# A late slot of at most 32 tokens, taken out of the list and computed in plain float32 beside another slot

## The chip, the cores and the metric

The kernel runs on one core of a Trainium2 chip. The metric is the device time of one execution in microseconds. Five engines work beside each other: PE (matrix products, with PEld loading the stationary operands), DVE, ACT and POOL (vector, activation and general work), and SP, whose queue issues most of the DMAs.

## The reference

An attention without a square of scores, whose output feeds a mixture of eight experts with one expert for each token. The batch is 8, with 8 heads, 576 positions and 64 channels a head, so 4,608 tokens of 512 channels.

```python
q_s = softmax(q, axis=-1);  k_s = softmax(k, axis=2)
kv = np.einsum('bhsd,bhse->bhde', k_s, v)
x = np.einsum('bhsd,bhde->bhse', q_s, kv)        # -> (4608, 512)
logits = xn @ en.T / tau                          # x and expert_emb normalized
expert_idx = np.argmax(logits, axis=1)
gate_w = softmax(logits)[arange(N), expert_idx]
for e in range(8):
    mask = expert_idx == e
    h = np.maximum(x[mask] @ w1[e], 0.0)          # w1[e]: 512 x 1024
    out[mask] = gate_w[mask, None] * (h @ w2[e])  # w2[e]: 1024 x 512
```

`softmax` stands for the exponentials less their maximum over their sum plus 1e-9. How many tokens an expert has is known only while the kernel runs.

## The kernel before

**Attention and routing.** Four groups of two batches are worked through in an order of small steps that is written out by hand (`ORDER`); each step is emitted when its name comes up, and every engine runs its own steps in that order. Step names that begin with `lp` are the instructions of the late plan, one DVE instruction each.

**Slots.** The tokens of one expert are computed in slots. Two direct slots and four early ones, 256 tokens each, run while the attention is still going on. What is left then is computed in late slots of up to three tiles of 128 tokens, expert after expert. The late plan (`late_plan`, lines 874 to 966) counts what each expert has left (`rem`), the tiles that make it up (`tiles`), the slots that these need (`ns`, tiles by three, rounded up), and for each slot in the list its expert, its first row and its count (`par`). An expert with a single token left has one tile and so one slot. The number of slots is `total`; the loop (lines 1373 to 1421) skips those behind it.

**One late slot.** Its products are made in split precision: every operand is cast to a rounded high part (ACT, line 1137) and a rest (DVE, line 1139), and three products of these stand for one. The first layer (`ffn1`, lines 1185 to 1187) runs over four quarters of the hidden units with 384 columns, or 256 where the slot has at most two tiles; 24 products a quarter. ACT and DVE (lines 1190 and 1192) make the two parts of the hidden values. The second layer (`ffn2`, lines 1207 to 1209) is 24 products of 512 columns for each tile that the slot has. ACT scales with the gate (line 1219) and POOL scatters the rows to the output (line 1221).

**What a slot prepares.** `fetch(...)[4]` is a row of functions: `[5]` reads the next slot's x rows in pieces (line 1088), `[7]` its first weights in four loads (line 1116), `[3]` its second weights in four (line 1126), `[4]` fills rows behind an expert's last one (line 1076). There is one buffer for raw first weights and one for raw second weights. So the first weights of the next slot are asked for when this slot's have all been split, ahead of its start; the second weights of the next slot go out one by one, as this slot's are split in its first layer. `split1` and `turnx` (block transposes of the x rows on DVE, and their split) are in `prepare` and `hidden`.

**PSUM in the late part.** Two buffers of tag `t`, two of `x` (first layer) and two of `po` (second layer).

Of the kernel before, what the change touches and what calls it, by code (L numbers as in the profile page):

```python
# [9 lines left out]
F32 = mybir.dt.float32  # L10
F32R = mybir.dt.float32r
BF16 = mybir.dt.bfloat16
I32 = mybir.dt.int32
# [10 lines left out]
P = 128  # L24
# [30 lines left out]
NMIN = -(-(N - TOOK_MAX) // T)  # L55
# [68 lines left out]
s4.3 lp6.3 lp7.3 lp9.3 lp8.3 gD.3 lp0.3 lp10.3 lp36.3 gE.3 s5.3 lp12.3 lp13.3 s6.3 lp29.3 pa43.4 lp11.3 lp14.3 lp15.3  # L124
lp16.3 lp17.3 pa42.4 pb42.4 hl41.4 hh42.4 hl42.4 pb43.4 hh43.4 hl43.4 lp18.3 lp19.3 lp20.3 lp21.3 lp22.3 lp23.3 lp27.3
lp37.3 lp25.3 lp26.3 lp28.3 lp30.3 lp35.3 lp24.3 lp33.3 lp31.3 lp34.3 sc6.3 po40.4 x5p1.4 sc3.3 od30.4 ob40.4 sc2.3
sc1.3 od31.4 sc7.3 sc4.3 lp32.3 sc8.3 sc5.3 x5p0.4 sc0.3 po41.4 x5h0.4 x5h1.4 ob41.4 od41.4 od40.4 x5l1.4 x5l0.4
right.4
# [4 lines left out]
def attention_moe(ctx, tc, q, k, v, emb, tau, w1, w2, out):  # L133
# [740 lines left out]
    def late_plan():  # L874
# [21 lines left out]
        st, ct = of_s[:, 2:3], of_s[:, 3:4]  # L896
        total = t([1], "total", I32)
# [7 lines left out]
        def spread():  # L905
# [15 lines left out]
            lambda: DVE.tensor_copy(ns, ni),  # L921
            lambda: DVE.scalar_tensor_tensor(nfull, ns, float(1 - TS), tiles, ALU.mult, ALU.add),
# [8 lines left out]
            lambda: DVE.tensor_tensor(i, slot_f, of_s[:, 0:1], ALU.subtract),  # L931
# [11 lines left out]
            lambda: DVE.tensor_scalar(bad, es, float(E), float(2 * ROWS), ALU.is_ge, ALU.mult),  # L943
            lambda: DVE.tensor_tensor(left, left, bad, ALU.add),
# [97 lines left out]
    def fetch(s, plan, i):  # L1042
# [30 lines left out]
        def pad():  # L1073
# [123 lines left out]
    def ffn2(s, j, got, bank="po", cuts=()):  # L1197

        ix = got[0]
        hh, hl = h_t["e" if s < EARLY - 1 else "l"]  # L1200
        ts_ = slice(j * P, (j + 1) * P)
        po = ps.tile([P, 2 * DM if bank == "x" else DM], F32, tag=bank, name=f"po{s}_{j}")[:, :DM]
        for c in range(NF):
            if c in cuts:
                yield
            for u in range(2):
                PE.matmul(po, hh[c][:, u, ts_], w2h[c][:, u, :], start=c + u == 0, stop=False)  # L1207
                PE.matmul(po, hh[c][:, u, ts_], w2l[c][:, u, :], start=False, stop=False)  # L1208
                PE.matmul(po, hl[c][:, u, ts_], w2h[c][:, u, :], start=False, stop=c + u == NC2 // 2)  # L1209
        yield  # L1210

        tag, bufs = ("et", 3) if s >= EARLY - 1 else (("mt", "kvd")[j], 1)
        ob = wk.tile([P, DM], F32, tag=tag, bufs=bufs, name=f"ob{s}_{j}")
# [17 lines left out]
        yield  # L1231

# [137 lines left out]
    got, total = last_early(), plans[-1][2]  # L1370
    open_banks("late")
    with ExitStack() as ifs:
        for s in range(EARLY, SLOTS):
# [80 lines left out]
```

## Time and profile before

| | |
|---|---|
| median of three runs | 588.98 us (584.9 to 590.15) |
| the profiled execution | 591.84 us |
| its span, first to last instruction | 590.0 us |
| mean granted clock of PE | 0.974 |
| PE busy | 531.2 us, 90% of the span |
| DVE, ACT, POOL busy | 352.2, 281.0, 204.4 us |
| expert weights loaded (`r`) | 96 loads of 512 KB |
| late tiles, of all 38 scattered | 26 |

How to read it. Times in the rows are microseconds from the span's start, if they are not marked ns. `L1185` is line 1185 of the kernel. PE's matmuls are pipelined: the start-to-start distance is the pace, and the duration of one is longer. A row of the timeline gives the start, the duration, the line and engine, the operation, out and in, and in brackets the idle time before it and what ended it. Where equal instructions follow one another, one row merges them (x64).

### The profile page before, as it was taken

To read this page: it belongs to the slowest core of one execution; us is meant where nothing else is said; L and a number is where in the kernel's file an instruction comes from. 1 tells how busy PE (TensorE), PEld (TensorE's weight loads), DVE (VectorE), ACT (ScalarE), POOL (GpSimd) and SP (SyncE) were. 2 spreads that over 40 slices of the span, in tenths; PEclk is the share of its full clock that TensorE was granted. 3 is DMA by queue.
4 is the path that set the end of the run, shared out by engine and by line. 5 is a ranking of instruction groups with operands and counts; after the bars stand their busy time and mean duration, and the time that the engine had idled before them with its cause. 6 is when DMAs were issued, how large, how long until landed. Compare 5 with 4: busy or idle time off the path is not lost. (4 is left out here: it accounts for less than half of the span.)

```text
span 590.0 us, 13113 instructions
## 1 busy us (share of the span) xinstructions
PE 531.2 (90%) x5068; PEld 476.3 (81%) x5068; DVE 352.2 (60%) x612; ACT 281.0 (48%) x423; POOL 204.4 (35%) x205
## 2 busy tenths in 40 slices
PE   1587887977599799999999998999999999999995
PEld 0476876876499687989998887989898989989894
DVE  4989989874465435644474758645547373645560
ACT  3459576724366426414453546344445353444450
POOL 1536428567248382174304133021131303031101
PEclk9989899989889999999999999999999999999998
DMA  9966925567563422059989687985674948485100
GB/s 317 391 222 203 323 86 183 170 214 255 201 189 107 154 91 75 2 209 308 281 261 207 204 197 209 254 187 189 158 218 121 240 127 229 140 198 188 46 19 33
DMA packets 65140, 109.23 MB, mean 185 GB/s; under 512 B 9918, under 2 KB 30942, under 8 KB 65056
## 3 DMA queue, kind: packets, MB, share of 16 engines
q1 hardware_dynamic: 55776, 85.76, 50.2%
q0 software_dynamic: 9200, 22.36, 11.0%
q8 instruction: 50, 0.82, 0.6%
q14 instruction: 34, 0.28, 0.2%
q10 hardware_dynamic: 80, 0.02, 0.0%
HBM read 88.66 MB, written 27.33 MB: 197 GB/s over the span
## 5 line engine op out<-in xcount | busy, mean ns | idle before, releaser
L1139 DVE TENSOR_TENSOR weights<-r,weights 128x1024 fp32r<-128x1024 f32 x92 | 117.3, 1291 | 72.5 <-ACT weights L1137 71.5
L1221 POOL DMA_INDIRECT out_dram<-ob,ix x34 | 37.2, 1095 | 241.8 <-ACT ob L1219 217.7
L1137 ACT CAST weights<-r 128x1024 fp32r<-128x1024 f32 x96 | 98.5, 1043 | 13.8 <-DMA r<-in_moe_w_dram 11.0
L1185 PE MATMUL ph<-x,weights 128*128 128x384 f32 (+1 forms) x320 | 102.3, 320 | 2.3 <-ACTq L1417 1.3
L1187 PE MATMUL ph<-x,weights 128*128 128x384 f32 (+1 forms) x320 | 102.2, 319 | 0.6 <-DVE weights L1139 0.6
L1186 PE MATMUL ph<-x,weights 128*128 128x384 f32 (+1 forms) x320 | 102.1, 319 | 0.1
L1208 PE MATMUL po<-weights,h_l 128*128 128x512 f32 x224 | 87.3, 390 | 0.0
L1209 PE MATMUL po<-weights,h_l 128*128 128x512 f32 x224 | 87.3, 390 | 0.0
L1207 PE MATMUL po<-weights,h_l 128*128 128x512 f32 x224 | 87.3, 390 | 0.0
L1192 DVE SCALAR_TENSOR_TENSOR h_l<-ph,h_l 128x768 fp32r<-128x768 f32 (+1 forms) x44 | 37.8, 860 | 47.7 <-ACT h_l L1190 47.4
L1190 ACT ACTIVATE h_l<-ph 128x768 fp32r<-128x768 f32 (+1 forms) x44 | 32.3, 734 | 66.4 <-PE ph L1187 58.1
L1185 PEld LDWEIGHTS ph<-x,weights 128*128 128x128 f32 x320 | 60.5, 189 | 3.6 <-ACTq L1417 1.7
L1185 PE MATMUL ph<-weights 128*128 128x256 f32 x192 | 58.1, 302 | 3.6 <-DVE h_most L1192 3.3
L1187 PEld LDWEIGHTS ph<-x,weights 128*128 128x128 f32 x320 | 60.5, 189 | 1.0 <-DVE weights L1139 1.0
L1186 PEld LDWEIGHTS ph<-x,weights 128*128 128x128 f32 x320 | 60.5, 189 | 0.5 <-issue 0.3
L1186 PE MATMUL ph<-weights 128*128 128x256 f32 x192 | 56.8, 296 | 1.7 <-issue 1.7
L1219 ACT ACTIVATE ob<-po,ix 128x512 f32<-128x512 f32 x34 | 23.3, 685 | 66.9 <-PE po L1209 53.3
L1209 PEld LDWEIGHTS po<-weights,h_l 128*128 128x128 f32 x224 | 42.0, 188 | 8.7
L1207 PEld LDWEIGHTS po<-weights,h_l 128*128 128x128 f32 x224 | 42.1, 188 | 8.5
L1208 PEld LDWEIGHTS po<-weights,h_l 128*128 128x128 f32 x224 | 42.1, 188 | 8.5
L819 POOL DMA_INDIRECT x_by_e<-x,posu x36 | 37.1, 1030 | 30.5 <-issue 8.1
L1187 PE MATMUL ph<-weights 128*128 128x256 f32 x144 | 42.7, 297 | 0.9 <-DVE weights L1139 0.9
(318 smaller groups left out, 957.0 us busy)
## 6 DMA issues: line engine op xcount, KB each, us to landing
r<-in_moe_w_dram SPq DMA_DIRECT2D x96, 512.0 KB, 6.8
k<-in_k_dram SPq DMA_DIRECT2D x6, 1152.0 KB, 7.9
q<-in_q_dram SPq DMA_DIRECT2D x6, 1152.0 KB, 5.3
v<-in_v_dram SPq DMA_DIRECT2D x6, 1152.0 KB, 13.3
xq<-x_by_e SPq DMA_DIRECT2D x36, 192.0 KB, 3.6
left<-in_v_dram SPq DMA_DIRECT2D x2, 1152.0 KB
left<-in_q_dram SPq DMA_DIRECT2D x2, 1152.0 KB, 10.9
left<-in_k_dram SPq DMA_DIRECT2D x1, 1152.0 KB, 7.8
```

The costliest lines, as they stand in the source:

```text
L819: ins = POOL.indirect_dma_start(x_by_e, bass.IndirectOffsetOnAxis(ap=posu[:, c : c + 1], axis=0), buf["x", g][:, j].bitcast(I32), None, bo ...
L1137: ACT.copy(hi, src)
L1139: eng.tensor_tensor(lo, src, hi.bitcast(F32), ALU.subtract)
L1185: PE.matmul(o, w1h[c][:, d, fs], xh[:, d, :n], start=d == 0, stop=False)
L1186: PE.matmul(o, w1h[c][:, d, fs], xl[:, d, :n], start=False, stop=False)
L1187: PE.matmul(o, w1l[c][:, d, fs], xh[:, d, :n], start=False, stop=d == NC1 - 1)
L1190: ACT.activation(hh[c][:, :, :n], ph[:, :, :n], AF.Relu)
L1192: DVE.scalar_tensor_tensor(hl[c][:, :, :n], ph[:, :, :n], 0.0, hh[c][:, :, :n].bitcast(F32), ALU.max, ALU.subtract)
L1207: PE.matmul(po, hh[c][:, u, ts_], w2h[c][:, u, :], start=c + u == 0, stop=False)
L1208: PE.matmul(po, hh[c][:, u, ts_], w2l[c][:, u, :], start=False, stop=False)
L1209: PE.matmul(po, hl[c][:, u, ts_], w2h[c][:, u, :], start=False, stop=c + u == NC2 // 2)
L1221: ins = POOL.indirect_dma_start(out, bass.IndirectOffsetOnAxis(ap=rows, axis=0), ob, None, bounds_check=N - 1, oob_is_err=False,)
```

## The change

The plan looks for the first expert whose rest is 1 to 32 tokens and takes its slot out of the list; that expert's first row, count and number go to the last line of the plan (`NSLOT - 1`), which was spare. Its tokens are computed in four pieces between the products of the fifth late slot (`FEW_AT = 4`), with the raw weights as they were loaded, without splitting:

- `load1`, `turn`: at the head of the fifth slot SP reads the 32 rows and the first weights into the one raw buffer, and DVE transposes the rows in 32x32 blocks. The next slot's first weights, which stood there, are moved behind `first`.
- `first`, behind the first quarter of the slot's first layer: 16 products, 4 over the channels by 4 column groups. Column group c writes 32 partitions of the output with quarter c of the hidden units, 256 columns. ACT applies the relu.
- `over_h`, behind the second quarter: two transposes and a copy.
- `second`, behind tile 0 of the second layer: 8 products of 512 columns, again in four column groups. ACT copies the four partial sums. The small expert's second weights are loaded (`load2`) where the next slot's were; the next slot's are moved behind `second`.
- `added`, behind the slot's last tile: one product with a matrix of ones and zeros adds the four groups, and the result goes out as any tile does.

The core of the diff (`send` is the end of the old `ffn2`, unchanged; in `ORDER` only names of `lp` steps change, since eight have been added):

```diff
+FEW, FEW_AT = 32, 4
-NMIN = -(-(N - TOOK_MAX) // T)
+NMIN = -(-(N - TOOK_MAX - FEW) // T)
...
             lambda: DVE.tensor_copy(ns, ni),
+            lambda: DVE.scalar_tensor_tensor(few, rem, float(FEW), tiles, ALU.is_le, ALU.mult),
+            lambda: DVE.scalar_tensor_tensor(back, exp_f, float(-E), few, ALU.add, ALU.mult),
+            lambda: DVE.tensor_reduce(first_few, back, AX.X, ALU.min),
+            lambda: DVE.scalar_tensor_tensor(few, back, first_few, few, ALU.is_equal, ALU.mult),
+            lambda: DVE.tensor_tensor(ns, ns, few, ALU.subtract),
+            lambda: DVE.tensor_scalar(last_row, slot_f, float(n - 1), None, ALU.is_equal),
+            lambda: DVE.tensor_scalar(others, slot_f, float(n - 1), None, ALU.is_lt),
...
+            lambda: DVE.scalar_tensor_tensor(es, first_few, last_row, es, ALU.mult, ALU.add),
...
+        def load1():
+            some = x_by_e[ds(first_row(2), T), :]
+            for c in range(NQ):
+                ins = SP.dma_start(rows[c * QB : (c + 1) * QB].bitcast(I32), some[:FEW, c * P : (c + 1) * P])
...
+            fetch(EARLY + i, plans[-1], i)[4][7]()
+
+        def load2():
+            fetch(EARLY + i, plans[-1], i)[4][3]()
...
+        def first():
+            t["ph"] = ps.tile([P, FC], F32, tag="t", name="ph_few")
+            for d in range(NC1):
+                for c in range(NF):
+                    PE.matmul(t["ph"][group[c]], x[:, d], r1[c][:, d, :], start=d == 0, stop=d == NC1 - 1)
+            ACT.activation(h, t["ph"], AF.Relu)
+
+        def over_h():
+            pt = ps.tile([P, us, P], F32, tag="t", name="pt_few")
+            for u in range(us):
+                PE.transpose(pt[:, u], h[:, u * P : (u + 1) * P], ident)
+            DVE.tensor_copy(turned, pt)
+
+        def second():
+            po = ps.tile([P, DM], F32, tag="po", name="po_few")
+            for u in range(us):
+                for c in range(NF):
+                    PE.matmul(po[group[c]], turned[:, u, group[c]], r2[c][:, u, :], start=u == 0, stop=u == us - 1)
+            ACT.copy(parts, po)
+
+        def added():
+            po = ps.tile([P, DM], F32, tag="po", name="sum_few")[:FEW]
+            PE.matmul(po, sums, parts, start=True, stop=True)
...
                     gn = fetch(nxt, plans[-1], i + 1)
+                    if i == FEW_AT:
+                        load1()
                     gn[4][5]()
-                    gn[4][7]()
+                    if i == FEW_AT:
+                        turn()
+                    else:
+                        gn[4][7]()
...
+                    if i + 2 == FEW_AT:
+                        fetch(EARLY + NSLOT - 1, plans[-1], NSLOT - 1)[4][4](1)
...
                     run(ffn1(s, nt, xs, c))
+                    if i == FEW_AT and c == 0:
+                        first()
+                        gn[4][7]()
+                    if i == FEW_AT and c == 1:
+                        over_h()
...
-                            gn[4][3]()
+                            (load2 if i == FEW_AT else gn[4][3])()
...
             run(ffn2(s, 0, got))
+            if i == FEW_AT:
+                second()
+                gn[4][3]()
...
+            if i == FEW_AT:
+                added()
```

Where the instructions stand now. On PE in the fifth late slot, at the end of the first layer's first quarter (`ph_3_0`, three tiles), before:

```order
L1185 MATMUL ph_3_0_5528<-x_3708,weights_355 128x384
L1186 MATMUL ph_3_0_5528<-x_3708,weights_355 128x384
L1187 MATMUL ph_3_0_5528<-x_3708,weights_355 128x384
L1185 MATMUL ph_3_1_5557<-x_3708,weights_355 128x384
L1186 MATMUL ph_3_1_5557<-x_3708,weights_355 128x384
```

and now (`r_3709` is the raw buffer of the first weights, `xg` the room of the small expert's rows):

```order
L1195 MATMUL ph_3_0_5550<-x_3716,weights_355 128x384
L1196 MATMUL ph_3_0_5550<-x_3716,weights_355 128x384
L1197 MATMUL ph_3_0_5550<-x_3716,weights_355 128x384
L1270 MATMUL ph_few<-r_3709,xg 32x256 x16
L1195 MATMUL ph_3_1_5604<-x_3716,weights_355 128x384
L1196 MATMUL ph_3_1_5604<-x_3716,weights_355 128x384
```

The sixteen float32 products stand ahead of the second quarter, which stood there directly.

On SP at the head of the fifth late slot and behind it (`xq` are x rows, `ix` their numbers, `r` first weights, `r_0` second weights), before:

```order
L1380 TENSOR_LOAD p_par
L1067 TENSOR_LOAD p_par
L1088 ISA
L1088 DMA xq<-x_by_e 32x12x128
...
L1093 DMA ix_114<-x_by_e 128x3x2
L1052 TENSOR_LOAD p_par
L1116 ISA
L1116 DMA r_3701<-in_moe_w_dram 32x4x1024
...
L1126 DMA r_0_3706<-in_moe_w_dram 128x2x512
```

and now:

```order
L1461 TENSOR_LOAD p_par
L1244 TENSOR_LOAD p_par
...
L1252 DMA xg<-x_by_e 32x128
...
L1254 DMA xg<-x_by_e 32x2
...
L1126 DMA r_3709<-in_moe_w_dram 32x4x1024
...
L1098 DMA xq<-x_by_e 32x12x128
...
L1126 DMA r_3709<-in_moe_w_dram 32x4x1024
...
L1136 DMA r_0_3714<-in_moe_w_dram 128x2x512
...
L1136 DMA r_0_3714<-in_moe_w_dram 128x2x512
```

The small expert's rows and first weights come first; the x rows of the next slot stand behind them, then the next slot's first weights, the small expert's second weights and the next slot's.

On PE behind tile 0 of the second layer of that slot, now (before, `po_1` followed `po_0` with the branch between them):

```order
L1306 MATMUL po_0_5861<-weights_677,h_l 128x512
L1283 MATMUL po_few<-r_0_3714,xg 32x512
L1283 MATMUL po_few<-r_1_3715,xg 32x512
L1283 MATMUL po_few<-r_2_3718,xg 32x512
L1283 MATMUL po_few<-r_3_3719,xg 32x512
...
L1513 COMPARE_AND_BRANCH
L1304 MATMUL po_1_5914<-weights_677,h_l 128x512
```

Eight products stand ahead of the branch to tile 1.

## Rows read from the trace of the kernel before

**Rows 1.** The page: busy time by engine, and PE's granted clock in 40 slices
```profile
PE 531.2 (90%) x5068; PEld 476.3 (81%) x5068; DVE 352.2 (60%) x612; ACT 281.0 (48%) x423; POOL 204.4 (35%) x205
...
PEclk9989899989889999999999999999999999999998
```

**Rows 2.** Waits of PE, 240 to 590 us (waiting line, releaser: us in total, times, longest)
```profile
PE ph L1185 <- ACTq L1417: 1.3, 1, 1.3
PE ph L1185 <- ACT weights L1137: 0.9, 1, 0.9
PE ph L1187 <- DVE weights L1139: 0.6, 1, 0.6
```

**Rows 3.** Timeline of PE (start us, us, line, operation, tiles, [idle before <- releaser])
```profile
342.71 0.36 PE L1185 MATMUL ph<-x,weights 128*128 128x256 f32 x1 [1.34 <-ACTq L1417]
...
354.62 0.40 PE L1207 MATMUL po<-weights,h_l 128*128 128x512 f32 x1
...
359.86 0.39 PE L1209 MATMUL po<-weights,h_l 128*128 128x512 f32 x1
361.16 0.45 PE L1185 MATMUL ph<-x,weights 128*128 128x384 f32 x1 [0.91 <-ACT weights L1137]
...
395.20 0.33 PE L1185 MATMUL ph<-x,weights 128*128 128x384 f32 x1
...
411.87 0.39 PE L1207 MATMUL po<-weights,h_l 128*128 128x512 f32 x1
...
428.23 0.33 PE L1185 MATMUL ph<-x,weights 128*128 128x384 f32 x1
```

**Rows 4.** Costliest groups, shapes apart: the plain float32 products of the attention
```profile
L625 PE MATMUL px<-kvx,et 64*64 64x73 f32 x1152 | 28.1, 240 | 5.4 <-DVE x L644 3.4 <-ACT et L615 0.9 <-DVE rq L641 0.7
```

**Rows 5.** Timeline of PE around such products, and eight transposes
```profile
232.99 0.28 PE L1187 MATMUL ph<-weights 128*128 128x256 f32 x1
233.20 1.36 PE L625 MATMUL px<-kvx,et 64*64 64x73 f32 x64
234.49 0.50 PE L1207 MATMUL po<-weights,h_most 128*128 128x512 f32 x1
...
254.62 1.03 PE L1158 MATMUL pt<-ident,xge 128*128 128x128 f32 x8
```

**Rows 6.** Timeline of the SP queue: DMA issues of one late slot and the next
```profile
382.96 1.92 SPq L1088 DMA_DIRECT2D xq<-x_by_e  x4
...
389.43 1.89 SPq L1116 DMA_DIRECT2D r<-in_moe_w_dram  x4
398.44 12.93 SPq L1126 DMA_DIRECT2D r<-in_moe_w_dram  x4
...
422.46 2.26 SPq L1116 DMA_DIRECT2D r<-in_moe_w_dram  x4
```

**Rows 7.** Line 1116 in 389:392 and in 422:426: time from issue to landing
```profile
DMA to landing us min/median/max: 5.2/7.1/9.1
...
DMA to landing us min/median/max: 10.2/10.2/10.2
```

**Rows 8.** Windows of a steady late slot (busy us by engine; clock, DMA share, GB/s)
```profile
415.00:417.00 2.00, 2.00 (x11) 1.65 (x10) 1.31 (x3) 1.01 (x2) 0.00 (x0) 1.00 0.09 10
...
sum 33.00, PE 33.00 PEld 30.16 DVE 17.04 ACT 14.39 POOL 6.90; mean PE 1.94 PEld 1.77 DVE 1.00 ACT 0.85 POOL 0.41
```

**Rows 9.** Timelines of DVE and POOL around the plan, and line 1158 on tile xg
```profile
251.52 0.20 DVE L934 TENSOR_SCALAR p_u<-p_u 20x2 f32<-20x2 f32 x1
251.59 0.14 DVE L935 TENSOR_TENSOR p_ft<-p_i,nxt_f 20x2 f32<-20x2 f32 x1
...
249.36 1.07 POOL L819 DMA_INDIRECT x_by_e<-x,posu  x1 [7.12 <-DVE p_of_s L930]
...
266.09 1.04 POOL L1059 DMA_INDIRECT xg<-x_by_e,late_place  x1 [0.30 <-DVE xq L961]
...
L1158 PE MATMUL pt<-ident,xg x12: 270/272/273, 281.6 to 282.8; 128*128 128x128 f32 x12
```

More of the change, by code (lines that the diff above doesn't have):

```diff
@@ L896, in late_plan @@
         st, ct = of_s[:, 2:3], of_s[:, 3:4]
+        few, back, first_few, last_row, others = se, ee[:, 0], u[:, 0:1], u[:, 1:2], ft[:, 0:1]
         total = t([1], "total", I32)
@@ L942, in late_plan @@
             lambda: DVE.tensor_tensor(ct, ct, ft[:, 0:1], ALU.subtract),
-            lambda: DVE.tensor_scalar(bad, es, float(E), float(2 * ROWS), ALU.is_ge, ALU.mult),
-            lambda: DVE.tensor_tensor(left, left, bad, ALU.add),
+            lambda: DVE.tensor_scalar(bad, es, float(E), float(ROWS), ALU.is_ge, ALU.mult),
+            lambda: DVE.tensor_tensor(st, st, bad, ALU.max),
             lambda: DVE.scalar_tensor_tensor(ct, bad, -1.0, ct, ALU.mult, ALU.add),
@@ L1071, in row_at, with pad @@
             return x_by_e[ds(first, T), :]
-        def pad():
+        def pad(nt=nt):
             for j in range(nt):
@@ L1195, in ffn1, with send @@
         yield
[L1197 to L1213, printed above, removed]
+    def send(s, ix, j, po, ob):
         if s < DIRECT:
@@ L1231, in ffn2, with few_parts, first_row, turn @@
         yield
+    def few_parts():
+        par, (place, over) = plans[-1][:2]
+        i, us = NSLOT - 1, FC // P
+        widths = dict(rows=P, x=NC1 * FEW, h=FC, turned=us * P, parts=DM, sums=FEW, ix=2)
+        room, at, end = xg_t[0].rearrange("p j x -> p (j x)"), {}, 0
+        for name, w in widths.items():
+            at[name], end = room[:, end : end + w], end + w
+        rows, x, h, turned, parts, sums, ix = at.values()
+        x, turned = x.rearrange("p (d n) -> p d n", d=NC1), turned.rearrange("p (u n) -> p u n", u=us)
+        ix = ix[:FEW].unsqueeze(1).bitcast(U32)
+        group = [slice(c * FEW, (c + 1) * FEW) for c in range(NF)]
+        r1, r2, r1_all = raws
+        t = {}
+        def first_row(k):
+            return nc.values_load(
+                par(k, i), engines=(mybir.EngineType.SP,), min_val=0, max_val=(E - 1, 0, ROWS)[k],
+                skip_runtime_bounds_check_because="clamped above",
+            )
+        def load1():
+            some = x_by_e[ds(first_row(2), T), :]
+            for c in range(NQ):
+                ins = SP.dma_start(rows[c * QB : (c + 1) * QB].bitcast(I32), some[:FEW, c * P : (c + 1) * P])
+                tc.add_to_no_dep_group("pieces", ins.ins)
+            ins = SP.dma_start(ix[:, 0].bitcast(I32), some[:FEW, DM:DX])
+            tc.add_to_no_dep_group("pieces", ins.ins)
+            fetch(EARLY + i, plans[-1], i)[4][7]()
+        def load2():
+            fetch(EARLY + i, plans[-1], i)[4][3]()
+        def turn():
+            DVE.tensor_reduce(sums, ident.rearrange("p (c n) -> p n c", n=FEW), AX.X, ALU.add)
+            DVE.transpose(x, rows.rearrange("p (d r) -> p d r", r=QB))
+            DVE.tensor_tensor(ix[:, :, 0], ix[:, :, 0], over[:FEW, i, 0:1], ALU.max)
+        def first():
[18 more added lines that the diff above has]
+            PE.matmul(po, sums, parts, start=True, stop=True)
+            ob = wk.tile([P, DM], F32, tag="et", bufs=3, name="ob_few")[:FEW]
+            run(send(SLOTS, ix, 0, po, ob))
+        return load1, load2, turn, first, over_h, second, added
@@ new lines, in ffn2 @@
+    def ffn2(s, j, got, bank="po", cuts=()):
+        ix = got[0]
+        hh, hl = h_t["e" if s < EARLY - 1 else "l"]
+        ts_ = slice(j * P, (j + 1) * P)
+        po = ps.tile([P, 2 * DM if bank == "x" else DM], F32, tag=bank, name=f"po{s}_{j}")[:, :DM]
+        for c in range(NF):
+            if c in cuts:
+                yield
+            for u in range(2):
+                PE.matmul(po, hh[c][:, u, ts_], w2h[c][:, u, :], start=c + u == 0, stop=False)
+                PE.matmul(po, hh[c][:, u, ts_], w2l[c][:, u, :], start=False, stop=False)
+                PE.matmul(po, hl[c][:, u, ts_], w2h[c][:, u, :], start=False, stop=c + u == NC2 // 2)
+        yield
+        tag, bufs = ("et", 3) if s >= EARLY - 1 else (("mt", "kvd")[j], 1)
+        ob = wk.tile([P, DM], F32, tag=tag, bufs=bufs, name=f"ob{s}_{j}")
+        yield from send(s, ix, j, po, ob)
@@ L1370, in attention_moe @@
     got, total = last_early(), plans[-1][2]
+    load1, load2, turn, first, over_h, second, added = few_parts()
     open_banks("late")
```

12 lines of the change are left out of this document (6 added, 6 removed).

## The prediction, made before the changed kernel ran

> **What bounds the kernel now.** I read the page first: PE's share and the clock line [rows 1]. PE is busy for 90% of the 590.0 us, and over the second half of the span its granted clock stands at 9 (90% or more) in every slice but the last, the 2.4 GHz level. Then PE's own waits in the part that the change touches, 240 to 590 us: three of them, 2.8 us together [rows 2]. So PE sets the pace of the late slots, and what the change is worth is PE's time taken out, less PE's time and new waits put in. The other engines have room there: in 33.0 us of a steady slot DVE is busy 17.0, ACT 14.4, POOL 6.9, and the DMA share falls to 0.09 before the next burst [rows 8]. The chain of waits on the page runs over the same products and tells nothing more.
>
> Next I cut the late part into slots at each first product of the first layer, in PE's timeline [rows 3]. A full slot of three tiles takes 428.23 - 395.20 = 33.03 us: first layer 411.87 - 395.20 = 16.67, then 5.44 for each tile. One slot, from 342.71 to 361.16, has only one burst of 24 second-layer products (354.62 to 359.86) before the next slot begins. It holds at most one tile. The inputs that the reference draws send 0, 582, 0, 1, 0, 2304, 1146 and 575 tokens to the eight experts. With 512 of the large expert's tokens taken at the start and 1,024 by the early slots, that gives late slots of 3+2, 1, 3+3, 3+3+3 and 3+2 tiles, ten in all, and the third is the one just seen: **one token costs a whole slot**. It is also the one that the new test (at most 32 tokens left) finds; the fifth late slot is then the first of the 1146.
>
> **The change part by part.** The sum goes against the profiled execution's 591.84 us, of which 590.0 are the span.
>
> *Removed.* The third slot goes, with what its shortness causes behind it (0.9 and 0.6 us of waits for split weights at its end [rows 2, 3]). The slot behind it began its steady run so that the one after starts at 395.20; without waits it would have started 33.03 earlier, at 362.17. In the new kernel the same three-tile slot takes the removed one's place at 342.71. I keep the 1.34 us wait ahead of 342.71 [rows 3]: it follows the second slot, which still has two tiles. Gain 362.17 - 342.71 = **19.46 us**.
>
> *Added on PE.* Sixteen float32 products of 32x256, eight of 32x512, one 32x512, two 128x128 transposes. The nearest rows are the attention's 64x73 products: 576 in the program, 1152 records [rows 4], so a plain float32 product is two records. 64 records, or eight sets of four products on four parts of the array, take 234.49 - 233.20 = 1.29 us [rows 5], 0.161 us a set. By columns a set of 256 is 0.565 us and one of 512 is 1.13. First layer four sets, 2.26; second two sets, 2.26; the adding product 1.13: 5.65 us. That price holds what is paid per instruction, so it is nearer an upper end for products that run side by side. Below, a record costs no less than a late product of its width: 24 take 5.24 us between first and last [rows 3], 0.228 each for 512 columns; two records each make 0.91 + 0.91 + 0.46 = 2.3 us. I take 5.65, since those rows are plain float32. The Trainium skill, page "FP8 and Floating Point Precision", section "TensorE Precision Notes", says that true float32 takes four passes through the array; at 0.228 us a pass that would be an estimate of 1.82 + 1.82 + 0.91 = 4.6 us, a sum 1.1 us lower, and it speaks against my lower end. No row here counts passes.
>
> Two transposes, by the row of eight in 1.03 us [rows 5]: 0.26 us.
>
> PE changes its tile shape six times (in and out of three pieces). Ahead of the attention's products the gap is 233.20 - 232.99 = 0.21 us, where the same product's pace is 0.12: 0.09 a change, 0.55 in all. The Trainium skill, page "TensorEngine Tiling (Array Packing)", section "Key Properties", says that a change of tiling mode drains the engine; a drained late product would show its 0.39 us instead of 0.228 [rows 3], an estimate of 0.16 a change and 1.0 in all. The row shows less, and I go by it.
>
> *Moved: the weights.* In before each slot asks for the next slot's first weights 5.8 us before its start (389.43 against 395.20) [rows 3, 6], and they have until the end of its first layer. Now the small expert's weights go there and are wanted after the first quarter, 4.17 us into the slot. The four issues end at about 391.0 and the last lands 9.1 us on, at 400.1, 4.9 into the slot; in the next slot issue to landing is 10.2, so 6.4 at most [rows 6, 7]. Wait 0.7 to 2.2 us; I take **1.3**. Loads land 1.9 us apart (5.2, 7.1, 9.1), one after another, so the x rows, now issued behind them instead of at 382.96 [rows 6], don't hold them up, and they are wanted only in the first layer's last quarter, 12.5 us into the slot.
>
> The next slot's first weights are now issued when the first piece is through, 4.17 + 1.3 + 2.3 = 7.8 us in, and land by 17 to 20; the casts that want them stand behind the first layer, at 16.67 + 1.3 + 2.3 + 0.3 = 20.6: covered. Behind them on the same queue come the small expert's second weights, four loads of 2 us, there by 25 to 28; the second piece wants them after tile 0, at 16.67 + 5.44 + 1.3 + 2.3 + 0.3 = 26.0. Wait 0 to 3; I take 0.5. The next slot's second weights leave at about 29 and have until that slot's own second layer, some 28 us later: covered.
>
> *ACT, DVE, POOL.* A relu of 128x256, copies of 128x256 and 128x512, a 32x32-block transpose, a reduction, one more fill and output: about 3 us in a slot with over 15 us free on each [rows 8]. ACT's copy of the second piece holds back two casts for the next slot by about 4 us; those are wanted in the second half of its first layer, over 20 us later. Cost 0; without that room PE would wait as it did at 361.16.
>
> *The plan.* Eight more small DVE instructions stand between the counts and the position numbers, at 0.07 to 0.20 us each [rows 9], by whether one waits for the last, about 1.2 us. Behind them wait POOL's scatters, then the gather at 266.09 and PE's transposes of the gathered rows at 281.6 [rows 9]. POOL works through from 249.36, so the gather slips by 1.2; 15.5 us lie between it and the transposes, and the slowest load of [rows 7] takes 10.2. The split passes of the early slot's last layer slip too, and PE uses the first of them soon after; I put 0.3 us, between 0 and 1.2.
>
> **Sum.** -19.46 + 5.65 + 0.26 + 0.55 + 1.3 + 0.5 + 0.3 = **-10.9 us**: 580.9 for the profiled execution. Its 591.84 is 2.86 over the median of the three runs (588.98; 584.9 to 590.15), so I forecast 588.98 - 10.9 = **578 us**, own range 572.5 (added work at 2.3, no waits) to 583 (waits at 2.2 and 3, the plan at 1.2, and 1 us for the runs' spread).
>
> **Rivals.** 1. *The four column groups don't run side by side.* The attention's products differ in rows and columns of the array; the new ones only in columns. For overlap: 0.161 us for four products is 40 ns each, while two records of 73 columns at the late pace would be 65, so something ran side by side; that columns alone suffice, no row shows. Then 16 x 0.565 + 8 x 1.13 + 1.13 = 19.2 us instead of 5.65, and the sum is +2.7: 591, down to 580 at the lower price of a record. Chance 0.10, half of it within 1%.
>
> 2. *PE starves for weights around the fifth slot.* It needs sixteen loads in about 40 us where a steady slot needs eight in 33 [rows 6]. If every load takes 10.2 us [rows 7] and the small expert's second weights come behind the next slot's first, PE waits 2.2 + 3 for the pieces and some 3 in the slot behind: -19.46 + 6.8 + 8.2 = -4.5, 584.5. Against it: the DMA share of 0.09 late in a slot [rows 8]. Chance 0.11, most of it within 1%.
>
> 3. *The small slot isn't taken out, and the time goes up.* The plan drops a slot only if its expert has at most 32 tokens left; with 33 or more the ten slots stay, and the four pieces run for nothing: +8.5 us, 597.5. Rows show only that the slot has one tile, up to 128 tokens; the one token comes from the reference's inputs. Chance 0.05.
>
> **How the numbers follow.** My forecast has 0.74. About 1% (5.9 us) is what a measurement of this kernel can tell from no change. Faster by more: 0.74 less 0.01, plus 0.04 of rival 1 and 0.03 of rival 2, is 0.80; slower by more: 0.05 and 0.01 of rival 1, 0.06; the rest, 0.14, within. The range takes in the forecast's own and the nearer halves of rivals 1 and 2: 572 to 585.
>
> **What the profile would show.** Nine late slots, the third starting at about 342.7 with 384 columns and followed at 375.7. In the fifth, the first piece's 32 records in about 2.3 us (9 if in series), a wait of 0.7 to 2.2 ahead of it for the small expert's first weights, under 1 ahead of the second piece. That slot should last 33.0 + 8.3 = 41.3 us, the slots behind it 33.0 again. A longer sixth slot speaks for rival 2; ten slots, for rival 3. I'm wrong if PE's other waits after 240 us grow by more than 3 us, or the pieces together take over 8.

## The result and the profile after

The changed kernel takes **580.2 us** (median of 20 runs, 576.4 to 583.8) against 586.3 (20 runs, 582.6 to 593.1) of the kernel before on the same chip: ratio 0.9893, 95% interval 0.9864 to 0.9923. That is 6.2 us less, between 4.5 and 8.0. The forecast was 578 us with a range of 572 to 585, and 10.9 us less. So direction and range held; the gain is a little over half of the one forecast. That the time itself came within 2.2 us of 578 is luck: the forecast's base, 588.98, was the median of three runs, and twenty runs of the same kernel give 586.3. Ratios and intervals are reckoned from the single runs, those of the chip's slower state left out, and are not quotients of the medians beside them.

The profiled execution took 580.45 us, span 578.6, mean granted clock 0.968. The lines of its page that answer to [rows 1]:

```profile
PE 521.9 (90%) x5000; PEld 463.3 (80%) x5000; DVE 333.4 (58%) x607; ACT 270.6 (47%) x411; POOL 201.8 (35%) x203
...
PEclk9988989899799899999999999999899999999997
```

PE has 9.3 us less to do. The clock line now has one 8 in its second half, near 413 us, and that slice is spoken of below. PE's timeline at the starts of the third to sixth late slot and of the one behind it, to be laid beside [rows 3]:

```profile
337.55 0.41 PE L1195 MATMUL ph<-x,weights 128*128 128x384 f32 x1 [1.06 <-ACTq L1513]
...
370.65 0.33 PE L1195 MATMUL ph<-x,weights 128*128 128x384 f32 x1
...
403.68 0.33 PE L1195 MATMUL ph<-x,weights 128*128 128x384 f32 x1
...
447.14 0.44 PE L1195 MATMUL ph<-x,weights 128*128 128x384 f32 x1
...
480.25 0.33 PE L1195 MATMUL ph<-x,weights 128*128 128x384 f32 x1
```

The third slot has 384 columns at once (three tiles) and is followed 33.10 us later: the one-token slot is gone. Nine slots run. The fifth takes 447.14 - 403.68 = **43.46 us** where the forecast had 41.3; the slot behind it takes 33.11. What happened inside the fifth, in PE's timeline, and the granted clock in windows of it (columns: window, length, PE busy, granted clock, DMA share, GB/s):

```profile
410.67 2.44 PE L1270 MATMUL ph_few<-r,xg 128*32 128x256 f32 x32 [2.63 <-DMA r<-in_moe_w_dram]
413.03 0.69 PE L1195 MATMUL ph<-x,weights 128*128 128x384 f32 x1
...
418.37 0.38 PE L1276 MATMUL pt_few<-ident,xg 128*128 128x128 f32 x2
418.50 0.42 PE L1195 MATMUL ph<-x,weights 128*128 128x384 f32 x1
...
433.16 1.92 PE L1283 MATMUL po_few<-r,xg 128*32 128x512 f32 x16
435.01 0.50 PE L1304 MATMUL po<-weights,h_l 128*128 128x512 f32 x1
...
446.16 1.04 PE L1288 MATMUL sum_few<-xg 128*32 128x512 f32 x2
```

```profile
411.00:412.00 1.00, 1.00 (x25) 0.98 1.10 319
412.00:413.00 1.00, 1.00 (x12) 0.50 1.16 157
...
414.00:415.00 1.00, 1.00 (x5) 0.50 0.80 201
415.00:416.00 1.00, 1.00 (x6) 0.81 1.10 274
```

From start to start the first piece takes 2.36 us, the second 1.85, the adding product 447.14 - 446.16 = 0.98, the transposes 0.13. PE waits 2.63 us for the small expert's first weights. From 412 us on, 1.3 us after PE is back, the granted clock stands at 0.50, that is 1.2 GHz and not 2.4, for some 3.4 us; the quarter from 413.03 to 418.37 takes 5.34 us instead of 4.17.

### The profile page after: what moved, and what is told of

The parts are those of the page before. It is cut to its first block, busy times and chain, and to the rows that moved or that the text cites. A ratio compares the mean times of both kernels' runs of the same rounds, so it can differ in the third digit from the quotient of the medians.

```text
span 578.6 us, 12866 instructions
## 1 busy us (share of the span) xinstructions
PE 521.9 (90%) x5000; PEld 463.3 (80%) x5000; DVE 333.4 (58%) x607; ACT 270.6 (47%) x411; POOL 201.8 (35%) x203
## 5 line engine op out<-in xcount | busy, mean ns | idle before, releaser
L1149 DVE TENSOR_TENSOR weights<-r,weights 128x1024 fp32r<-128x1024 f32 x84 | 103.0, 1242 | 79.2 <-ACT weights L1147 76.4
L1216 POOL DMA_INDIRECT out_dram<-ob,ix x33 | 35.8, 1086 | 234.4 <-ACT ob L1214 209.8
L1147 ACT CAST weights<-r 128x1024 fp32r<-128x1024 f32 x88 | 90.3, 1044 | 15.8 <-DMA r<-in_moe_w_dram 13.9
L1195 PE MATMUL ph<-x,weights 128*128 128x384 f32 (+1 forms) x288 | 94.0, 326 | 1.1 <-ACTq L1513 1.1
L1197 PE MATMUL ph<-x,weights 128*128 128x384 f32 (+1 forms) x288 | 93.4, 324 | 0.0
L1196 PE MATMUL ph<-x,weights 128*128 128x384 f32 (+1 forms) x288 | 93.4, 324 | 0.0
L1304 PE MATMUL po<-weights,h_l 128*128 128x512 f32 x216 | 84.4, 391 | 0.4 <-issue 0.4
L1305 PE MATMUL po<-weights,h_l 128*128 128x512 f32 x216 | 84.2, 390 | 0.0
L1306 PE MATMUL po<-weights,h_l 128*128 128x512 f32 x216 | 84.2, 390 | 0.0
L1202 DVE SCALAR_TENSOR_TENSOR h_l<-ph,h_l 128x768 fp32r<-128x768 f32 (+1 forms) x40 | 34.9, 875 | 49.3 <-ACT h_l L1200 49.2
L1200 ACT ACTIVATE h_l<-ph 128x768 fp32r<-128x768 f32 (+1 forms) x40 | 29.9, 747 | 66.2 <-PE ph L1197 57.8
L1195 PE MATMUL ph<-weights 128*128 128x256 f32 x192 | 56.4, 294 | 1.7 <-DVE h_most L1202 1.7
L1195 PEld LDWEIGHTS ph<-x,weights 128*128 128x128 f32 x288 | 54.7, 190 | 3.6 <-ACTq L1513 1.5
L1196 PE MATMUL ph<-weights 128*128 128x256 f32 x192 | 55.0, 287 | 1.3 <-issue 1.3
L1196 PEld LDWEIGHTS ph<-x,weights 128*128 128x128 f32 x288 | 54.8, 190 | 0.2
L1197 PEld LDWEIGHTS ph<-x,weights 128*128 128x128 f32 x288 | 54.6, 190 | 0.0
L1304 PEld LDWEIGHTS po<-weights,h_l 128*128 128x128 f32 x216 | 40.6, 188 | 9.7 <-ACT ob L1214 0.8
L1306 PEld LDWEIGHTS po<-weights,h_l 128*128 128x128 f32 x216 | 40.5, 188 | 8.5
L1305 PEld LDWEIGHTS po<-weights,h_l 128*128 128x128 f32 x216 | 40.6, 188 | 8.1
L1197 PE MATMUL ph<-weights 128*128 128x256 f32 x144 | 41.2, 286 | 0.2 <-DVE weights L1149 0.2
## 6 DMA issues: line engine op xcount, KB each, us to landing
left<-in_q_dram SPq DMA_DIRECT2D x2, 1152.0 KB, 10.9
```

The lines of the kernel that those rows point to most:

```text
L1147: ACT.copy(hi, src)
L1149: eng.tensor_tensor(lo, src, hi.bitcast(F32), ALU.subtract)
L1195: PE.matmul(o, w1h[c][:, d, fs], xh[:, d, :n], start=d == 0, stop=False)
L1196: PE.matmul(o, w1h[c][:, d, fs], xl[:, d, :n], start=False, stop=False)
L1197: PE.matmul(o, w1l[c][:, d, fs], xh[:, d, :n], start=False, stop=d == NC1 - 1)
L1200: ACT.activation(hh[c][:, :, :n], ph[:, :, :n], AF.Relu)
```

## The experiments

Times of other chips differ by some 2%, so each kernel is held against the kernel before on its own chip. Slots and stretches are read from one trace each.

**1. Without the pieces.** The constant that names the slot is set to one that never comes.

```
-FEW, FEW_AT = 32, 4
+FEW, FEW_AT = 32, -9
```

> Leaves out the small expert's four pieces and their loads (its one token isn't computed); the plan's eight instructions and the removed slot stay as in the change. Theory: all that the pieces cost lies in the fifth late slot, 43.46 us there against 33.0 to 33.1 of its neighbours. Then the fifth slot takes 33.0 to 33.1, the granted clock stays at 0.97 to 1.00 in it, and the time is about 10.4 us under the changed kernel's: some 570 by the 20-run median of 580.2. Rival 1: part of the pieces' cost lies elsewhere, in the stretch behind the last scatter's issue (8.72 us after the change, 6.08 before) for one, since one more output row block is sent; then that stretch falls to about 6.1 and the time is 13 us under. Rival 2: the slot in the neighbours' place would have been slow without the pieces too; then the fifth slot stays over 35.

Measured: 579.7 us against 597.4 of the kernel before on this chip, ratio 0.9707 (0.9681 to 0.9734). Against the change's 0.9893 that is 0.0186 of 597.4, 11.1 us less. The starts of the fifth and sixth slot in PE's timeline:

```profile
413.47 0.33 PE L1195 MATMUL ph<-x,weights 128*128 128x384 f32 x1
...
446.49 0.33 PE L1195 MATMUL ph<-x,weights 128*128 128x384 f32 x1
```

33.02 us: all that the pieces cost lies in their slot, 10.4 us in the first trace of the change. (The small expert's one token isn't computed in this kernel.) The stretch behind the last scatter's issue stays at 8.65 us, so rival 1 falls: that growth comes with nine slots, pieces or not.

**2. The first piece one quarter later.**

```
-                    if i == FEW_AT and c == 0:
+                    if i == FEW_AT and c == 1:
                         first()
                         gn[4][7]()
-                    if i == FEW_AT and c == 1:
+                    if i == FEW_AT and c == 2:
                         over_h()
```

> The first piece stands behind the second quarter of the fifth late slot's first layer and not the first, the two transposes behind the third; nothing else. Theory: PE's 2.63 us wait for the small expert's first weights, and the fall of the granted clock to 0.5 behind it (the next quarter took 5.34 us and not 4.17), are both the price of asking for the weights too late. 4.17 us more of products ahead of the piece cover the wait, so the clock stays at 1.00, and the fifth slot takes 43.46 - 2.63 - 1.17 = 39.7 us: the time falls by 3.8 us. Rival 1: it is the 32-row float32 products that bring the clock down, wait or no wait; then the wait goes, the quarter behind the piece still takes 5.3 us, the slot 40.8. Rival 2: the next slot's first weights, which are asked for when the first piece is through, now leave 1.5 us later than in the change and come too late for their casts; then a wait for split weights of 1 to 4 us stands at the end of the fifth slot or in the sixth, and the time falls by less than 2 us.

Measured: ratio 0.9881 (0.9849 to 0.9912), no different from the change's 0.9893. The fifth slot takes 43.29 us. The theory holds for the first piece, the wait and the clock both, and yet nothing is won; PE's timeline at the two pieces:

```profile
423.51 1.93 PE L1270 MATMUL ph_few<-r,xg 128*32 128x256 f32 x32
425.38 0.44 PE L1195 MATMUL ph<-x,weights 128*128 128x384 f32 x1
...
439.33 0.39 PE L1306 MATMUL po<-weights,h_l 128*128 128x512 f32 x1
440.41 1.04 PE L1283 MATMUL po_few<-r,xg 128*32 128x512 f32 x2 [0.69 <-DMA r<-in_moe_w_dram]
441.76 1.05 PE L1283 MATMUL po_few<-r,xg 128*32 128x512 f32 x2 [0.30 <-DMA r<-in_moe_w_dram]
443.12 1.05 PE L1283 MATMUL po_few<-r,xg 128*32 128x512 f32 x2 [0.31 <-DMA r<-in_moe_w_dram]
444.44 1.90 PE L1283 MATMUL po_few<-r,xg 128*32 128x512 f32 x10 [0.28 <-DMA r<-in_moe_w_dram]
446.27 0.50 PE L1304 MATMUL po<-weights,h_l 128*128 128x512 f32 x1
```

No wait ahead of the first piece, the clock at 1.00 in every window of the slot, the piece 1.87 us. But PE comes to the second piece at 439.56, 24.5 us into the slot and not 29.5 as in the change (28.35 in the change's second trace, experiment 6), and the small expert's second weights land one by one until 444.4, 29.4 us into it. The second piece takes 446.27 - 439.56 = 6.71 us instead of 1.85: waits, and three products alone at 1.05 us each, since the other groups' weights aren't there and nothing runs beside them. They weren't asked for late: the last of the four was issued 18.1 us into the slot here and 22.4 in the change, and landed at 29.4 here and 28.3 there. None of the three theories had this: **the wait at the first piece had been the cover of the second piece's loads**.

**3. The plan alone.** The pieces are left out as in experiment 1, and no slot is taken out.

```
-DVE.scalar_tensor_tensor(few, rem, float(FEW), tiles, ALU.is_le, ALU.mult)
+DVE.scalar_tensor_tensor(few, rem, 0.0, tiles, ALU.is_le, ALU.mult)
```

> The plan's eight added instructions alone: the test asks for at most 0 tokens left, so no slot is removed, ten late slots stay, and the four pieces and their loads are left out; all tokens are computed as before the change. Theory (the forecast's term): the plan costs 0.3 us, between 0 and 1.2, so the time is that of the kernel before, up to 0.3 us over it. Rival: the pair of traces, where the stretch from the plan's route product to the first late slot is 1.35 us longer after the change, shows its price; then the time is 1.3 us over the kernel before, with a wait of about 1 us on PE ahead of an early slot's second layer. The stretch behind the last scatter's issue tells whether its 2.64 us of growth belong to the plan (8.7 here) or not (about 6.1).

Measured: ratio 1.0010 (0.9984 to 1.0036), 0.6 us slower, between 1.0 faster and 2.1 slower: the runs can't tell 0.3 from 1.3. The trace can. From the route's product (`pre`) to the first late slot, first in the kernel before, then here:

```profile
242.95 0.33 PE L749 MATMUL pre<-ohe,ones 128*128 128x72 f32 x2
...
285.70 0.41 PE L1185 MATMUL ph<-x,weights 128*128 128x384 f32 x1
```

```profile
246.79 0.34 PE L750 MATMUL pre<-ohe,ones 128*128 128x72 f32 x2
...
290.68 0.41 PE L1195 MATMUL ph<-x,weights 128*128 128x384 f32 x1
```

It takes 43.89 us, where the kernel before took 42.75. The stretch behind the last scatter's issue is 6.25, as before: its growth isn't the plan's.

**4. The column groups in turn.** In both pieces the loops change places, so that products of one column group follow one another.

```
-            for d in range(NC1):
-                for c in range(NF):
+            for c in range(NF):
+                for d in range(NC1):
...
-            for u in range(us):
-                for c in range(NF):
+            for c in range(NF):
+                for u in range(us):
```

> The same 24 float32 products of the first and second piece, in another order: all of one column group's products, then all of the next group's, so that neighbouring products nearly always want the same columns of the array. Theory: the pieces are cheap because four products on four column groups run side by side, a set of four 512-column products in 0.93 us and one single product of that width in 0.98. In this order three of four go, so the first piece takes up to 16 x 0.49 = 7.8 us and not 2.4, the second up to 8 x 0.95 = 7.6 and not 1.85, and the fifth slot 54 us and not 43.5. Rival: a product of 32 columns of the array costs less by itself (a quarter of the array, a quarter of the time); then both pieces keep their 2.4 and 1.9 us.

Measured in one run: fifth slot 44.85 us. The first piece in PE's timeline:

```profile
419.25 4.57 PE L1270 MATMUL ph_few<-r,xg 128*32 128x256 f32 x32 [2.55 <-DMA r<-in_moe_w_dram]
423.75 0.45 PE L1195 MATMUL ph<-x,weights 128*128 128x384 f32 x1
```

It takes 4.50 us at a granted clock of 1.00 throughout, against 1.87 of the same products in the change's order at that clock. So the order counts, and rival (a narrow product is cheap by itself) falls: only products of different groups run side by side. But the theory's sizes fall too: the second piece, in which each group has two products in a row, keeps its 1.9 us, and the first pays 2.6 us more and not 5. A picture that fits both: a group can hold one product that runs and one that waits, and the third in a row holds up what is behind it. With 1.87 / 4 = 0.47 us a product the first piece would then take 3 x 0.94 + 1.88 = 4.7, the second what it took. That picture wasn't tested.

**5. Both pieces later.** Experiment 2's edit, and the second piece behind the second tile.

```
             run(ffn2(s, 0, got))
+            prepare(range(2, NF), False)
             if i == FEW_AT:
-                second()
-                gn[4][3]()
-            prepare(range(2, NF), False)
-            with ExitStack() as more:
                 for j in range(1, TS):
-                    more.enter_context(tc.If(cnt > j * P))
-                    run(ffn2(s, j, got))
-            if i == FEW_AT:
+                    with tc.If(cnt > j * P):
+                        run(ffn2(s, j, got))
+                    if j == 1:
+                        second()
+                        gn[4][3]()
                 added()
...
```

The other slots keep the old loop. The casts for the next slot (`prepare`) come ahead of the second piece with this, too.

> The first piece stands behind the second quarter of the fifth late slot's first layer (as in the run before), and the second piece, with the load of the next slot's second weights behind it, stands after the second tile of the second layer and not after the first. Theory: what is late are the loads, and each piece must stand where its weights have landed: with the first piece moved alone, the second waited for its weights until 29.4 us into the slot; after tile 1 PE gets there at 29.9, so no wait is left at either piece. The slot takes 33.0 + 1.9 + 0.1 + 1.9 + 1.0 and some 0.9 for changes and gaps, 38.8 to 39.4 us against 43.46, and the time falls by 4 us under the changed kernel's. Rival 1: the next slot's weights are late now, since they leave behind the pieces and the slot is 4 us shorter; then the fifth slot is 39 us but a wait of 1 to 4 us stands in the sixth, and less than 2 us is won. Rival 2: the loads queue up longer and the second piece still waits; then the slot stays over 41.

Measured: **576.3 us against 589.2 of the kernel before on this chip, ratio 0.9805** (0.9756 to 0.9854). The slot in PE's timeline:

```profile
402.97 0.33 PE L1195 MATMUL ph<-x,weights 128*128 128x384 f32 x1
...
411.41 1.93 PE L1270 MATMUL ph_few<-r,xg 128*32 128x256 f32 x32
...
432.98 1.92 PE L1283 MATMUL po_few<-r,xg 128*32 128x512 f32 x16
...
441.52 0.44 PE L1195 MATMUL ph<-x,weights 128*128 128x384 f32 x1
```

No wait at either piece; the second is reached 30.0 us into the slot. The slot takes 38.55 us, 0.25 under the lower end of what was expected, and the slot behind it 33.11, so rivals 1 and 2 fall. This is the fastest of the kernels here that compute every token.

**6. The changed kernel again, on the chip of experiment 5.**

> The changed kernel again, on the chip of the other runs of this call. Theory 1: a wait of 2.6 us at the first piece always makes the granted clock fall to 0.5 behind it; then this trace shows it again, the quarter behind the piece takes 5.3 us and the slot 43.5. Theory 2: the fall belongs to that one execution (in the trace of the kernel with the groups in turn the same wait of 2.55 us left the clock at 1.00); then it may be missing here, the first piece takes 1.9 us, the quarter 4.2 and the slot 41.8. The stretch from the route's product to the first late slot should be 43.9 to 44.5 as in the five traces with the new plan, the stretch behind the last scatter's issue 8.7.

Measured: 581.8 us, ratio 0.9888 (0.9851 to 0.9925); experiment 5 is 5.5 us under it by the medians and 4.9 by the ratios, of which the traces of the slot show 3.8. Its fifth slot, and the clock behind the wait:

```profile
406.58 0.33 PE L1195 MATMUL ph<-x,weights 128*128 128x384 f32 x1
...
413.65 1.93 PE L1270 MATMUL ph_few<-r,xg 128*32 128x256 f32 x32 [2.73 <-DMA r<-in_moe_w_dram]
415.52 0.45 PE L1195 MATMUL ph<-x,weights 128*128 128x384 f32 x1
...
429.26 0.50 PE L1304 MATMUL po<-weights,h_l 128*128 128x512 f32 x1 [0.73 <-issue]
...
448.91 0.44 PE L1195 MATMUL ph<-x,weights 128*128 128x384 f32 x1
```

```profile
414.00:415.00 1.00, 1.00 (x28) 1.00 1.09 317
415.00:416.00 1.00, 1.00 (x15) 1.00 1.19 178
```

The same wait, and the clock stays up: theory 1 falls. The slot takes 42.33 us. The row at 429.26 is a wait that no theory had: 0.73 us ahead of the second layer's first product, put down to nothing that the profile shows. All five traces with the first piece in its old place have it, with 0.39 to 0.89 us (0.39 in the first trace of the change); experiments 1, 2 and 5 haven't. What makes it stays open.

**7. The kernel before again.**

> The kernel before again. Theory: the plan's eight instructions cost 1.2 us; then the stretch from the route's product to the first late slot is 42.7 here as in the first trace of this kernel, with no wait ahead of the early slot's second layer. Rival: the 42.75 was one execution's luck; then it is 43.9 or so here. The stretch behind the last scatter's issue should be 6.1, as in both traces with ten slots.

Measured in one run, span 592.8 us: 42.96 from the route's product to the first late slot, with 0.18 us of wait in that stretch, so the plan's price stands (below). Behind the last scatter 6.17. New is how much the removed slot can cost: third and fourth slot take 20.23 + 35.62 = 55.85 us and not 52.49 [rows 3]. There are 1.86 us of idle time in the third, put down to nothing that the profile shows, and behind the waits for split weights the clock falls in this kernel too:

```profile
364.00:365.00 1.00, 1.00 (x5) 0.59 1.15 327
365.00:366.00 1.00, 1.00 (x5) 0.50 1.13 188
```

**8 and 9. The stretch behind the last scatter.** First the changed kernel written out for 18 late slots and not 19, then the changed kernel with one slot fewer run.

```
-NMAX = (N - TOOK_MIN + E * (T - 1)) // T
+NMAX = (N - TOOK_MIN + E * (T - 1)) // T - 1
```

> The changed kernel written out for at most 18 late slots and not 19; nine of them run, as in the change. The stretch behind the last scatter's issue is 8.65 to 8.75 us in all four traces of kernels that run nine slots, with the pieces or without, and 6.1 to 6.25 in the two that run ten. Theory: it goes by how many slots are written out behind the last one and skipped (ten with nine run, nine with ten run): with nine skipped here the stretch is 6.1. Rival: it goes by the slot that is the last to run, the ninth or the tenth, whose buffers alternate: then it is 8.7 here. The rest as in the changed kernel.

```
-DVE.tensor_copy(total, cum[:, E - 1 : E])
+DVE.tensor_scalar(total, cum[:, E - 1 : E], -1.0, None, ALU.add)
```

> The changed kernel, told that there is one late slot less than the plan lists: eight run, and the ninth slot's tokens aren't computed. The number of skipped slots didn't set the stretch behind the last scatter's issue (8.75 us with nine run and nine skipped). Theory: it goes by the last slot's place, odd or even, whose buffers and output queue entries alternate: the tenth gives 6.1 to 6.25, the ninth 8.65 to 8.75, so the eighth should give about 6.2. Rival: it grows with each slot that is not run, by whatever the engines have to pass at the end: then 8.7 or more, up to 11. The rest as in the changed kernel: the fifth slot 42.3 or, where the granted clock falls to 0.50 behind the wait, 43.2 to 43.5.

Measured: 8.75 us in the first (span 578.8, last issue 570.05), so the number of skipped slots isn't it. In the second 6.72. The last issue in POOL's timeline, of the kernel before (span 590.0), of the change (578.6) and of experiment 9 (557.3):

```profile
583.92 0.97 POOL L1221 DMA_INDIRECT out_dram<-ob,ix  x1 [4.41 <-ACTq L1417]
```

```profile
569.88 0.97 POOL L1216 DMA_INDIRECT out_dram<-ob,ix  x1 [4.42 <-ACTq L1513]
```

```profile
550.58 0.97 POOL L1216 DMA_INDIRECT out_dram<-ob,ix  x1 [4.46 <-ACT ob L1214]
```

6.08, 8.72 and 6.72 us to the end. Over all traces: ten slots 6.1 to 6.25, nine 8.65 to 8.75, eight 6.7. That speaks against growth with each slot not run. Odd against even isn't shown either: eight is 0.5 over what was expected, and experiment 9 differs in a second way, since its last slot has three tiles and that of the others two. No engine is busy behind the last scatter, but the instructions that POOL's queue itself runs can be read. They include a DRAIN (count, then shortest, median and longest in ns); before, after, experiment 9:

```profile
L1449 POOLq DRAIN  x3: 46/107/879, 588.3 to 589.8; - x3
```

```profile
L1547 POOLq DRAIN  x3: 46/107/2431, 575.4 to 578.4; - x3
```

```profile
L1547 POOLq DRAIN  x3: 46/107/2022, 554.5 to 557.1; - x3
```

The longest, 0.88 us before and 2.43 after, makes 1.55 of the 2.64 us of growth; a semaphore instruction ahead of it (INC_SWDGE_SEM, 0.38 and 0.76) makes 0.38 more. In the kernels of eight and nine slots the DRAIN goes with the number of DMAs that POOL has issued: 2.02 us with 108, 2.27 with 111 (experiment 1), 2.43 with 113, 0.082 us for each. The kernel before has 115 and 0.88, so that number alone doesn't set it, and what makes ten slots cheaper stays open. In passing, the clock fell behind the first piece's wait in experiment 8 (fifth slot 44.07 us) and not in 9 (42.28).

## Why the prediction was right, and where its sizes were off

Two pairs of traces, terms in us; the second pair is experiments 6 and 7, of one chip:

| step | forecast | first pair | second pair |
|---|---|---|---|
| third slot removed, with the stall behind it | -19.46 | -19.39 | -22.75 |
| fifth slot: pieces, changes, waits | +8.26 | +10.43 | +9.30 |
| the plan (route's product to first slot) | +0.3 | +1.35 | +0.96 |
| second slot | 0 | -0.29 | -0.35 |
| behind the last scatter's issue | none | +2.64 | +2.58 |
| sum | -10.9 | -5.26 | -10.26 |
| the traces, route's product to the end | | -5.18 | -10.15 |

The sums close to 0.1 us. Between them lie single executions; the medians of many runs say -6.2 and -6.6 (-8.8 to -4.4). What comes before the route's product isn't touched by the change, and differed by 6.2 us in the first pair and 2.3 in the second: so a difference of two spans says little here, and a difference of stretches more.

**Removed.** Right to 0.1 us in the first pair, by laying slot starts side by side. In two of three traces with ten slots the stall behind the short slot also cost 1.6 us of half clock (35.6 instead of 34.04 in experiments 3 and 7), which the forecast couldn't see in one trace: the removal is worth 19.4 to 22.8 us.

**The pieces' own time: right, the range better than the value.** 1.87 + 1.85 + 0.98 = 4.70 us without waits and at the full clock, against 5.65. The set of four products of 512 columns takes 0.93 us, the lone adding product 0.98: the groups run side by side, rival 1 is out. The prediction cited the Trainium skill, page "FP8 and Floating Point Precision", section "TensorE Precision Notes", on four passes and the estimate of 4.6 us from it. The trace agrees: 0.93 is 4 x 0.23, the late products' pace of [rows 3]. What the 73-column products of [rows 4, 5] pay for each instruction doesn't carry over to 256 and 512 columns. The changes of shape: experiment 5's slot is 5.52 us over 33.03, less 4.70 and 0.13 for the transposes leaves 0.69, 0.11 for each of six, against 0.09 forecast.

**The wait for the first weights: mis-sized, by a misread row.** 2.6 to 2.8 us in all five traces with the piece in its place, where 1.3 was forecast and 2.2 was the upper bound. The issues went out as forecast, 5.78 us ahead of the slot. But the last of the four was under way for 10.8 us, by the chain of waits:

```profile
399.50 10.82 DMA r<-in_moe_w_dram
410.31 0.35 issue
```

The forecast took 9.1, with 10.2 as the bound [rows 7]. The row 5.2/7.1/9.1 there holds only two landings, since the trace of before knows them for two of the four issues; 9.1 is the third load's, and 7.1 the mean of both. The third load alone, before and after, and the fourth of another slot of the kernel before (issued at 490.2):

```profile
DMA to landing us min/median/max: 9.1/9.1/9.1
```

```profile
DMA to landing us min/median/max: 8.8/8.8/8.8
```

```profile
DMA to landing us min/median/max: 10.6/10.6/10.6
```

Where the two traces of the kernel before know the fourth load's landing, from 360 us on, it took 10.2 to 10.7 us. With that the wait comes to 1.8 to 2.3 us, and to 2.2 to 2.7 with the 0.35 between landing and product: nearly all that was measured. The x rows, which go out right behind these loads now, aren't needed to explain it. The third load landed no later for them (8.8 against 9.1), the fourth at most 0.6 later.

**The wait ahead of the second piece: none, for a reason that the forecast missed.** It added two waits as if they stood apart. Experiment 2 shows that they share one cause, the loads: what PE doesn't wait for at the first piece it waits for at the second, unless that is moved as well. Rival 2 had the mechanism (PE starves for weights around the fifth slot), but put part of its price into the slot behind, which never waited.

**Half the clock, and a wait that nobody forecast.** The forecast had no such terms. Half the clock costs 1.2 us in the quarter behind the piece and 0.5 in the piece itself (2.36 against 1.87) in the first trace of the change, and nothing in the second. The unexplained wait ahead of the second layer costs 0.4 and 0.7 us. That is why the fifth slot came out over the forecast although its pieces were cheaper: 4.70 + 0.13 + 0.69 + 2.73 + 0.73 = 8.98 of the 9.30 us in the second trace.

**The plan: mis-sized.** The stretch takes 43.9 to 44.5 us in nine traces with the new plan, 42.75 and 42.96 in two without; by the medians 1.1 us. The prediction put it at 0.3, since 15.5 us lay between the gather and its use. The gather isn't where it shows. It is the early slot's last layer, which the prediction named and priced low (PE's waits in the stretch):

```profile
245.13 0.50 PE L1306 MATMUL po<-weights,h_most 128*128 128x512 f32 x1 [0.20 <-DVE h_most L1202]
250.72 0.50 PE L1304 MATMUL po<-weights,h_most 128*128 128x512 f32 x1 [0.77 <-ACT ob L1214]
```

These make 0.75 to 1.0 us in each trace with the new plan, and at most 0.2 in those without.

**Behind the last scatter: the step that the sum lacked.** 2.6 us, in the first pair nearly as much as all other errors together, and the largest single reason that a gain of 10.9 became 6.2: -10.9 + 2.6, + 0.8 for the plan, + 1.0 to 2.2 for the fifth slot makes -5.3 to -6.5. A row of the trace of before could have shown the 6.08 us; nothing in it shows that they would grow. Over half of the growth is the DRAIN of POOL's queue (experiments 8 and 9).

## What to carry to other kernels

Where work is slipped between other work and brings its own loads, find when each load lands and put each piece behind that moment; taking one wait away alone may only hand it to the next piece on the same queue, as experiment 2 did, while moving both made the slot 3.8 us shorter (42.33 to 38.55). Sum the change over stretches between fixed events to the very end of the span, the tail behind the last instruction included. A row of least, median and most speaks only for the issues whose landing the trace knows; ask for each issue by itself before a wait is priced by the last. Order products on different column groups of the array alternately: four in a row on one group cost 2.6 us here, two cost nothing, and three were not run.

## What the runs showed of the hardware that was not expected

- The granted clock can fall to 0.50 for 3.4 us behind 1.5 to 2.8 us of idle PE, in some executions and not in others: behind the first piece's wait in two of five traces, behind the short slot's stall (0.91 + 0.64 us) in two of three. Each fall cost 1.5 to 1.6 us of its slot, once the waits that differ between the traces are taken off. What decides it stays open.
- Four plain float32 products with 32 columns of the stationary operand each, on four column groups, take as long as one (0.93 against 0.98 us at 512 columns), and two in a row on one group cost nothing more where four groups are in use.
- Behind the issue of the last output this program takes 6.1 to 8.75 us more with no engine busy. Most of the difference is in POOL's own queue, whose DRAIN took 0.88 us with ten slots run, and 2.02 to 2.43 with eight or nine, there 0.082 us more for each DMA that POOL had issued.
- The four loads of 512 KB that go out together ahead of a late slot land one after another: from 360 us on, but for the slot behind the small expert's, they took 4.8 to 5.4, 6.7 to 7.8, 8.6 to 9.2 and 9.7 to 10.8 us from their own issues, in the kernel before as in the changed one.
